# Layer norm 2's root by Pool as a power, a new interleave over four PSUM slots, and down sums in another order

## The chip, the cores and the metric

The kernel runs on one core of a Trainium2 chip. The metric is the device time of one execution in microseconds (us). PE is the tensor engine, DVE the vector engine, ACT the scalar engine, POOL the GpSimd engine, SP the engine that issues most DMAs. A profile's span is about 2 us shorter than the time of the same execution.

## The reference

```python
x = A_x                                            # 2048 x 576
h = x + spectral(layernorm(x), A_w_r, A_w_i)       # 2-D FFT, filter, inverse FFT, to bf16
h2 = h + (gelu(n @ w_gate) * (n @ w_up)) @ w_down  # n = layernorm(h); 4608 hidden columns
```

Layer norm has eps = 1e-5 and no weights.

## The kernel before: the parts that matter here

The 2048 rows are 16 tiles of 128. The program is recorded operation by operation: each engine runs its operations in the order of recording, and the recorder adds the semaphore waits. The spectral part ends with an inverse transform. For a tile `c`, `I` makes a half-transformed tile in PSUM (six matmuls) and ACT moves it to `GS`; `N` multiplies by the second table (four matmuls) and DVE adds it to the residual `XO`, with the row sum as accumulator:

```python
def st_N(c):
    ...                                                    # 4 matmuls into two PSUM banks
    P.op(DVE, ... scalar_tensor_tensor(x2, banks(...), 1.0, x2, op0=mult, op1=add,
                                       accum_out=SB2[:, 0, c:c + 1]), ...)
```

Eight tiles are inverted before the feed-forward part starts. Layer norm 2 of the first block (tiles 0 to 3, in the groups 0-2 and 3) needs sums, squares (ACT, `sq`), a root, the norm itself, and a transpose by matmul ("turn") into `HT`. Its root was taken on two engines, and the sequence was written by hand:

```python
def ln2_b(q):   # ACT
    a.activation(RS2[:, c0:c1], RS2[:, c0:c1], ACTF.Sqrt, bias=EPT[:, 0:1])
def ln2_c(q):   # DVE
    v.reciprocal(RS2[:, c0:c1], RS2[:, c0:c1])

# ... cut: I0 to s2
ln2_a(0); st_I(5); ln2_b(0); st_N(4); sq(3); ln2_c(0)
norm(0, DVE); norm(1, POOL); norm(2, POOL)
ln2_a(1); st_I(6); ln2_b(1); st_N(5); st_I(7); ln2_c(1); norm(3, DVE)
turn_pe(0, ACT); st_N(6); turn_pe(1, DVE); turn_pe(2, ACT); turn_pe(3, ACT); st_N(7)
```

A PSUM slot is two banks. Inverses and turns alternated between slots 0 and 1, `N` steps between slots 2 and 3. After that come four blocks of 512 rows. Each has 36 gate/up steps `f` (18 matmuls, then Gelu on ACT and a product on DVE into `AT`), and then the down sums over `f`. In blocks 1 to 3 the gate/up steps run in the order 9 to 35, then 0 to 8, but the sums ran from 0 to 35:

```python
for h, (d0, d1) in enumerate(((0, cut), (cut, D))):
    b = (0, 1, 2, 3)[2 * (p % 2) * (tb > 0) + h]
    ...
    for f in range(36):
        ...
        t.matmul(bank(b, 0, 128, 0, d1 - d0), AT[:, f, ...], WD[:, f, d0:d1], start=(f == 0), stop=(f == 35))
    P.op(DVE, ... tensor_tensor(OS[...], bank(b, ...), XO[:, c, d0:d1], op=add), ...)
```

Of the kernel before, what the change touches and what calls it, by code (L numbers as in the profile page):

```python
# [5 lines left out]
F32 = mybir.dt.float32  # L6
# [8 lines left out]
NT = 16  # L15
# [2 lines left out]
NPAIR = 18  # L18
EPS = 1e-5
NPRE = 8  # L20


def _np_bf16(a):
# [286 lines left out]
def _build(nc, A_x, A_w_r, A_w_i, B_w_gate, B_w_up, B_w_down, out):  # L310
# [40 lines left out]
    TM = sb.alloc("TM", [128, 2, NT], F32)  # L351
    RS2 = sb.alloc("RS2", [128, NT], F32)
    EPT = sb.alloc("EPT", [128, 1], F32)
    OS = sb.alloc("OS", [128, 2, D], BF16)
    shared = (sb.off + 63) // 64 * 64

# [42 lines left out]
    def banks(b, n, w):  # L399
        return PS[:, b * 512:(b + n) * 512].rearrange("p (a c) -> p a c", a=n)[:, :, 0:w]  # L400


    P.op(POOL, lambda g: g.memset(ZD[:, :], 0.0), w=["ZD"])
    P.op(POOL, lambda g: g.memset(EPT[:, :], EPS), w=["EPT"])
    P.op(POOL, lambda g: g.memset(WS[:, :, :, 0:KW:K2], 0.0), w=["Wz"])
    xv = A_x[0].rearrange("(p c) d -> p c d", c=NT)
# [353 lines left out]
    vkeys = vk[0] + vk[1] + vk[2]  # L760


    ISEQ = [("I", c) for c in range(8)] + [("T", i) for i in range(4)]
    seq = {k: i % 2 for i, k in enumerate(ISEQ)}

    def islot(c):
        return seq["I", c]

    def i_mm(c, h, i):
        b, kt = 2 * islot(c) + h, 2 * i + h  # L770
        P.op(PE, lambda t, b=b, h=h, i=i, kt=kt, c=c: t.matmul(bank(b, 0, 128, 0, K2), V[:, c, kt, :, :], DT[:, 3 * h + i, 0:K2],  # L771
                                                              start=(i == 0), stop=(i == 2)), r=vk[i] + ["DT"], w=[("PS", b)])

    def i_ev(c):
        sl, b0 = c % 2, 2 * islot(c)
        if c == 0:
            P.op(DVE, lambda v, sl=sl, b0=b0: v.tensor_copy(GS[:, sl, 0, 0:K2], bank(b0, 0, 128, 0, K2)), r=[("PS", b0)], w=[("G", sl, 0)])
            P.op(ACT, lambda a, sl=sl, b0=b0: a.activation(GS[:, sl, 1, 0:K2], bank(b0 + 1, 0, 128, 0, K2), ACTF.Copy), r=[("PS", b0 + 1)], w=[("G", sl, 1)])
        else:
            P.op(ACT, lambda a, sl=sl, b0=b0: a.activation(GS[:, sl, :, 0:K2], banks(b0, 2, K2), ACTF.Copy),  # L780
                 r=[("PS", b0), ("PS", b0 + 1)], w=[("G", sl, 0), ("G", sl, 1)])


    def st_I01():
        for c in range(2):
            for h in range(2):
                i_mm(c, h, 0)
        for c in range(2):
            for h in range(2):
                for i in (1, 2):  # L790
                    i_mm(c, h, i)
            i_ev(c)
# [11 lines left out]
    def st_N(c):  # L804
        sl = c % 2
        for h in range(2):
            b = 4 + 2 * sl + h
            for i in range(2):
                rhs = GS[:, sl, i, 288:0:-1] if h else GS[:, sl, i, 0:288]
                P.op(PE, lambda t, b=b, h=h, i=i, c=c, rhs=rhs: t.matmul(bank(b, 0, 128, 0, 288), IT[:, h * i, c, :], rhs, start=(i == 0), stop=(i == 1)),  # L810
                     r=[("G", sl, i), "IT"], w=[("PS", b)])
        x2 = XO[:, c, 0:D].rearrange("p (a b) -> p a b", a=2)
        P.op(DVE, lambda v, x2=x2, c=c, sl=sl: v.scalar_tensor_tensor(x2, banks(4 + 2 * sl, 2, 288), 1.0, x2, op0=ALU.mult, op1=ALU.add,  # L813
                                                               accum_out=SB2[:, 0, c:c + 1]),
             r=[("PS", 4 + 2 * sl), ("PS", 5 + 2 * sl)], w=[("X", c), ("S0", c)])


    QR = ((0, 3), (3, 4), (4, NPRE), (NPRE, NT))

    def ln2_a(q):  # L820
        c0, c1 = QR[q]
        P.op(DVE, lambda v, c0=c0, c1=c1: v.tensor_scalar(TM[:, 1, c0:c1], SB2[:, 0, c0:c1], -1.0 / D, None, op0=ALU.mult), r=[("S0", c) for c in range(c0, c1)], w=[("MN", q)])
        P.op(DVE, lambda v, c0=c0, c1=c1: v.tensor_tensor(TM[:, 0, c0:c1], TM[:, 1, c0:c1], TM[:, 1, c0:c1], op=ALU.mult), r=[("MN", q)], w=[("M2", q)])
        P.op(DVE, lambda v, c0=c0, c1=c1: v.scalar_tensor_tensor(RS2[:, c0:c1], SB2[:, 1, c0:c1], 1.0 / D, TM[:, 0, c0:c1], op0=ALU.mult, op1=ALU.subtract),
             r=[("M2", q)] + [("S1", c) for c in range(c0, c1)], w=[("V2", q)])

    def ln2_b(q):
        c0, c1 = QR[q]
        P.op(ACT, lambda a, c0=c0, c1=c1: a.activation(RS2[:, c0:c1], RS2[:, c0:c1], ACTF.Sqrt, bias=EPT[:, 0:1]), r=[("V2", q), "EPT"], w=[("SD2", q)])

    def ln2_c(q):
        c0, c1 = QR[q]
        P.op(DVE, lambda v, c0=c0, c1=c1: v.reciprocal(RS2[:, c0:c1], RS2[:, c0:c1]), r=[("SD2", q)], w=[("RS2", q)])

    def lq(c):
        return sum(c >= q0 for q0, _ in QR) - 1
# [17 lines left out]
    def turn_pe(c, eng):  # L854
        hs = c % 4
        t0, t1 = 128 * c, 128 * c + 128
        b0 = 2 * seq["T", c]
        for k in range(5):
            b, o = b0 + k // 4, 128 * (k % 4)
            lhs = HN[:, hs, 128 * k:128 * k + 128]  # L860
            P.op(PE, lambda t, b=b, o=o, lhs=lhs: t.matmul(bank(b, 0, 128, o, o + 128), lhs, IDT[:, :], start=True, stop=True),
                 r=[("HN", hs, 0), ("HN", hs, 1), "IDT"], w=[("PS", b)])
        dst, src = HT0[:, 0:5, t0:t1], PS[:, b0 * 512:b0 * 512 + 640].rearrange("p (k e) -> p k e", k=5)
        fn = (lambda a: a.activation(dst, src, ACTF.Copy)) if eng == ACT else (lambda v: v.tensor_copy(dst, src))  # L864
        P.op(eng, fn, r=[("PS", b0), ("PS", b0 + 1)], w=[("HT", 0, c, 0)])

    def sq(c):
        square(c, OS[:, c % 2, :], ("OS", c % 2, 0))

    st_I01()  # L870
    st_N(0)
    st_I(2)
    st_N(1)
    sq(0)
    st_I(3)
    st_N(2)
    sq(1)
    st_I(4)
    st_N(3)
    sq(2)  # L880
    ln2_a(0)
    st_I(5)
    ln2_b(0)
    st_N(4)
    sq(3)
    ln2_c(0)
    norm(0, DVE)
    norm(1, POOL)
    norm(2, POOL)
    ln2_a(1)  # L890
    st_I(6)
    ln2_b(1)
    st_N(5)
    st_I(7)
    ln2_c(1)
    norm(3, DVE)
    turn_pe(0, ACT)
    st_N(6)
    turn_pe(1, DVE)
    turn_pe(2, ACT)  # L900
    turn_pe(3, ACT)
    st_N(7)

    P.alias(ukeys + [(n_, a) for n_ in ("CU", "SU") for a in range(3)], [("WD", j) for j in range(9)])
    for j in range(9):
# [68 lines left out]
    def down(tb, p):  # L974
        c = 4 * tb + p

        cut = 448 if c == NT - 1 else 288
        for h, (d0, d1) in enumerate(((0, cut), (cut, D))):
            b = (0, 1, 2, 3)[2 * (p % 2) * (tb > 0) + h]
            cd = NPRE + 2 * p + h if tb == 0 else NT  # L980
            if cd < NT:
                def_i(cd)
            for f in range(36):
                if cd < NT and f == 22:
                    def_n(cd)
                P.op(PE, lambda t, b=b, d0=d0, d1=d1, f=f, p=p: t.matmul(bank(b, 0, 128, 0, d1 - d0), AT[:, f, 128 * p:128 * p + 128],  # L986
                                                                        WD[:, f, d0:d1], start=(f == 0), stop=(f == 35)),
                     r=[("AT", f), ("WD", f // 4)], w=[("PS", b)])
            P.op(DVE, lambda v, b=b, d0=d0, d1=d1, p=p, c=c: v.tensor_tensor(OS[:, p % 2, d0:d1], bank(b, 0, 128, 0, d1 - d0), XO[:, c, d0:d1], op=ALU.add),  # L989
                 r=[("PS", b), ("X", c)], w=[("OS", p % 2, k) for k in (range(2) if d1 == cut and cut > 288 else (h,))])  # L990
            P.dma(SP, ov[:, c, d0:d1], OS[:, p % 2, d0:d1], f"so{p % 2}{h}", r=[("OS", p % 2, h)], w=[("OUT", p % 2, h)])


    P.alias(fdead, fnew)
    for tb in range(4):
        for f in range(36):
            gu_part(36 * tb + f, False)
            if f:
                gu_part(36 * tb + f - 1, True)
            if tb == 0 and f == 10:  # L1000
                wg_load(3, 0)
            if tb == 0 and f < NPRE - 4:
                sq(4 + f)
            if tb == 0 and f == 8:
                ln2_a(2)
                ln2_b(2)
                ln2_c(2)
            f0, f1 = (15, 3) if tb == 0 else (2, 4)
            if tb < 3 and f >= f0 and (f - f0) % f1 == 0 and (f - f0) // f1 < 4:
                norm(4 * (tb + 1) + (f - f0) // f1)  # L1010
                turn_dma(4 * (tb + 1) + (f - f0) // f1)
        gu_part(36 * tb + 35, True)
        for p in range(4):
            down(tb, p)
        if tb == 0:
            ln2_a(3)
            ln2_b(3)
            ln2_c(3)
            P.alias(vkeys + ["DP", "ITD", "EB", "Q0", "Q1", "YB0", "YB1", "JD"], [("WG", 3, k) for k in range(4)])
            wg_load(0, 3)  # L1020
    P.op(SP, None, r=[("OUT", i, h) for i in range(2) for h in range(2)])
# [36 lines left out]
```

## Time and profile before

Time before: 501.41 us, median of 3 runs (501.16 to 501.94); with a fourth run, 501.5. I cut the span by marks that the chain of waits and the timeline show: the first matmul of the inverse transform, the first gate/up matmul, and the start of each later block. The last come from the chain of waits and lie up to 0.07 us after a block's first matmul; block 1 before is counted from its second matmul, the first that had to wait.

| part of the span before | from, to (us) | length |
|---|---|---|
| up to the first inverse matmul | 0 to 53.16 | 53.16 |
| transition: inverse, layer norm 2, turns | 53.16 to 67.21 | 14.05 |
| block 0 | 67.21 to 179.36 | 112.15 |
| blocks 1, 2, 3 | 179.36, 285.41, 391.39 to 497.49 | 106.05, 105.98, 106.10 |

From the page of the kernel before: span, busy time by engine, and the chain of waits summed by engine.

```profile
span 499.7 us, 9895 instructions
PE 487.6 (98%) x4322; PEld 290.5 (58%) x4323; DVE 197.3 (39%) x431; ACT 159.4 (32%) x299; POOL 37.4 (7%) x51
PE 88%; DVE 8%; issue 2%; ACT 1%; DMA 1%; DVEq 0%; ACTq 0%
```

PE is busy nearly all the time, so only its gaps can be won. The chain of waits of the kernel before, in order of time (start, length, engine, tile, line, count), shows where it left PE:

```profile
59.26 0.77 DVE XO L813 x2
...
61.39 1.08 DVE HN L842 x2
...
65.08 0.75 DVE HT L864
65.87 0.47 PE PS L861 x5
66.36 0.71 ACT HT L864
67.08 0.14 issue
67.21 70.11 PE PS L936 x648
...
178.84 0.47 DVE OS L989
179.36 70.11 PE PS L936 x647
249.56 0.61 ACT GL L945
250.19 0.70 DVE AT L946
250.93 34.47 PE PS L986 x280
```

The reader should see three places: the transition (to 67.21), an output add before block 1 (178.84), and a Gelu and a product inside a down sum (249.56), which comes back at the other two blocks. PE's own waits in the same trace (who waited for whom, us in total, times, longest) for the lines concerned:

```profile
PE PS L986 <- DVE AT L946: 1.2, 3, 0.4
PE PS L861 <- DVE HT L864: 0.8, 1, 0.8
PE PS L936 <- DVE OS L989: 0.3, 1, 0.3
```

These waits are shorter than the time lost, since a matmul's recorded end is modelled and lies after its last issue. Eight matmuls at 0.123 us from 249.39 end their issue at 250.37; the ninth started at 250.93. So 0.55 us is lost there, where the view says 0.4.

### The profile page before, as it was taken

The numbers are of one execution on the slowest core, as the hardware profiler recorded it, in microseconds if no ns is written. First come the engines' busy times: TensorE is split into PE (matmuls) and PEld (weight loads), VectorE is DVE, ScalarE is ACT, GpSimd is POOL, SyncE is SP. The second block draws the span as 40 slices with busy tenths as digits, with TensorE's granted clock in tenths as the row PEclk, the third lists the DMA queues.
The fourth block names the chain that finished last, engine by engine and source line by source line (L and its number), as shares of the span: only waits on it lengthen the run. The fifth ranks groups of instructions, "written<-read, shape, count | busy, mean of one in ns | idle before, by whom it ended". The sixth has DMA issues, their size and how long they took to land.

```text
span 499.7 us, 9895 instructions
## 1 busy us (share of the span) xinstructions
PE 487.6 (98%) x4322; PEld 290.5 (58%) x4323; DVE 197.3 (39%) x431; ACT 159.4 (32%) x299; POOL 37.4 (7%) x51
## 2 busy tenths in 40 slices
PE   6999989999999999999999999999999999999998
PEld 2688745555588854444477744444577544444775
DVE  5899743443365544433311134433210233333111
ACT  7888765332321242323300023323100133233000
POOL 3653260000000010000000000000000000000000
PEclk9899999999999999999999999999999999999999
DMA  8765796511000052100000001100000000000000
GB/s 281 169 206 183 253 354 250 210 26 26 7 13 13 14 182 65 25 9 1 2 13 19 18 14 22 20 1 1 7 12 19 13 1 1 1 2 1 12 19 19
DMA packets 27163, 31.32 MB, mean 63 GB/s; under 512 B 11664, under 2 KB 19984, under 8 KB 27120
## 3 DMA queue, kind: packets, MB, share of 16 engines
q1 hardware_dynamic: 24224, 18.75, 13.0%
q0 software_dynamic: 2896, 11.95, 6.8%
q8 instruction: 34, 0.56, 0.5%
q14 instruction: 9, 0.07, 0.1%
HBM read 26.35 MB, written 2.36 MB: 57 GB/s over the span
## 4 chain that ended last, share of the span: by engine, by line
PE 88%; DVE 8%; issue 2%; ACT 1%; DMA 1%; DVEq 0%; ACTq 0%
PE PS L936 56%; PE PS L986 28%; DVE TP L667 2%; DVE ST L468 1%; PE PS L953 1%; PE PS L771 1%; DVE ZS L672 1%; DVE CUS L641 1%; PE PS L691 1%; DMA XO<-in_A_x_dram 1%; DVE XO L813 1%; PE PS L628 1%; DVE U L533 0%; DVE AT L946 0%; PE PS L810 0%
## 5 line engine op out<-in xcount | busy, mean ns | idle before, releaser
L936 PE MATMUL PS<-HT,WG 64*128 64x512 bf16 x2106 | 229.1, 376 | 0.7 <-ACT HT L864 0.4
L936 PEld LDWEIGHTS PS<-HT,WG 64*128 64x128 bf16 x2106 | 107.7, 94 | 120.4 <-issue 1.4
L946 DVE TENSOR_TENSOR AT<-GL,PS 128x512 bf16<-128x512 bf16 x144 | 99.0, 688 | 176.4 <-ACT GL L945 176.4
L945 ACT ACTIVATE GL<-PS 128x512 bf16<-128x512 f32 x144 | 85.9, 597 | 258.5 <-PE PS L936 246.4
L986 PE MATMUL PS<-WD,AT 128*128 128x288 bf16 (+2 forms) x1152 | 144.8, 286 | 1.2 <-DVE AT L946 1.2
L986 PEld LDWEIGHTS PS<-WD,AT 128*128 128x128 bf16 x1152 | 110.5, 98 | 32.6 <-DVE AT L946 2.1
L989 DVE TENSOR_TENSOR OS<-PS,XO 128x288 bf16<-128x288 f32 (+2 forms) x32 | 14.6, 458 | 102.0 <-PE PS L986 102.0
L936 PE MATMUL PS<-HT,WGX 64*128 64x512 bf16 x486 | 53.8, 376 | 0.0
L936 PEld LDWEIGHTS PS<-HT,WGX 64*128 64x128 bf16 x486 | 23.8, 94 | 28.8
L712 POOL TENSOR_SCALAR WS<-WS 128x290 bf16<-128x290 bf16 x16 | 15.4, 963 | 9.2 <-DMA WS<-in_A_w_i_dram 5.4
L628 PE MATMUL PS<-FT,U 128*128 128x290 bf16 x96 | 14.4, 287 | 0.5 <-DVE U L533 0.5
L801 ACT ACTIVATE JD<-XO 128x576 bf16<-128x576 bf16 x8 | 5.5, 683 | 28.5 <-DVE XO L970 28.5
L667 DVE TENSOR_TENSOR TP<-YS,WS 128x580 bf16<-128x580 bf16 (+2 forms) x32 | 13.4, 459 | 0.3 <-issue 0.3
L691 PE MATMUL PS<-VT,ZS 128*128 128x256 bf16 x102 | 13.5, 272 | 0.0
L704 ACT ACTIVATE V<-PS 128x768 bf16<-128x768 f32 x15 | 12.0, 811 | 0.8 <-PE PS L691 0.6
L660 ACT ACTIVATE YS<-PS 128x578 bf16<-128x578 f32 x16 | 10.5, 655 | 3.5 <-PE PS L657 3.3
L657 PE MATMUL PS<-CUS,BT 128*128 128x289 bf16 (+2 forms) x96 | 10.7, 246 | 0.3 <-DVE CUS L641 0.3
L522 PE MATMUL PS<-ATS,XO 128*128 128x128 bf16 (+1 forms) x80 | 7.3, 238 | 3.8 <-POOL ATS L495 2.3
L628 PEld LDWEIGHTS PS<-FT,U 128*128 128x128 bf16 x96 | 9.2, 98 | 3.0 <-issue 0.6
L691 PEld LDWEIGHTS PS<-VT,ZS 128*128 128x128 bf16 x102 | 9.2, 98 | 1.8 <-DVE ZS L672 0.2
L468 DVE BATCH_NORM_STATS2 ST<-XO 128x6 f32<-128x288 bf16 x22 | 8.4, 445 | 3.8 <-DMA XO<-in_A_x_dram 3.8
L657 PEld LDWEIGHTS PS<-CUS,BT 128*128 128x128 bf16 x96 | 8.3, 97 | 2.1 <-issue 0.5
(75 smaller groups left out, 201.2 us busy)
## 6 DMA issues: line engine op xcount, KB each, us to landing
WD<-in_B_w_down_dram POOLq DMA_DIRECT2D x9, 576.0 KB, 11.6
WG<-in_B_w_up_dram SPq DMA_DIRECT2D x4, 1152.0 KB, 6.6
WG<-in_B_w_gate_dram POOLq DMA_DIRECT2D x4, 1152.0 KB, 9.8
out_dram<-OS SPq DMA_DIRECT2D x30, 72.0 KB, 1.6
XO<-in_A_x_dram SPq DMA_DIRECT2D x3, 576.0 KB, 7.3
WGX<-in_B_w_gate_dram POOLq DMA_DIRECT2D x1, 1152.0 KB, 6.7
WGX<-in_B_w_up_dram SPq DMA_DIRECT2D x1, 1152.0 KB, 11.1
HT<-HN SPq DMA_TRANSPOSE x60, 2.4
```

Of the source, the lines that this page charges most:

```text
L468: P.op(DVE, lambda v, c=c, h=h: v.bn_stats(ST1[:, c, h, :], XO[:, c, 288 * h:288 * h + 288]), r=[("X", c)], w=[("ST1", c, h)])
L628: P.op(PE, lambda t, b=b, o=o, dt=dt, us=us, g=g: t.matmul(bank(b, 0, 128, 0, 2 * HK), U[:, us, g, :, :], FT[:, o, dt, :], start=(dt == 0) ...
L657: P.op(PE, lambda t, b=b, tb=tb, pl=pl, q0=q0, q1=q1, m=m, s3=s3, sp_=sp_: t.matmul(bank(b, 0, 128, q0, q1), BT[:, sp_, tb, :], CUS[:, s3, ...
L667: P.op(DVE, lambda v: v.tensor_tensor(out, YS[:, sl, :, q0:q1], WS[:, g, w_, q0:q1], op=ALU.mult), r=[("Y", sl), ("Wn", i), "Yz", "Zz"] + ...
L691: P.op(PE, lambda t, b=b, o=o, zp=zp, lhs=lhs, sp_=sp_, m=m, n=len(parts): t.matmul(bank(b, 0, 128, o, o + 256), lhs, VT[:, sp_, zp, :], s ...
L704: P.op(ACT, lambda a, dst=dst, src=src: a.activation(dst, src, ACTF.Copy), r=[("PS", bs[0]), ("PS", bs[2])], w=[("V", g, c) for c in range ...
L712: P.op(POOL, lambda v, g=GORD[i]: v.tensor_scalar(WS[:, g, 0, :], WS[:, g, 2, :], -1.0, None, op0=ALU.mult), r=[k for k in wkeys[0 if 1 <= ...
L936: op = P.op(PE, lambda t, h0=h0, kt=kt, wt=wt, b=b, s=(not second and j == 0), e=(second and j == n - 1): t.matmul(bank(b), wg_tile(slot)[ ...
L945: P.op(ACT, lambda a: a.activation(GL[:, s2, :], bank(b0), ACTF.Gelu_apprx_tanh), r=[("PS", b0)], w=[("GL", s2)])
L946: P.op(DVE, lambda v: v.tensor_tensor(AT[:, f, :], GL[:, s2, :], bank(b0 + 1), op=ALU.mult), r=[("GL", s2), ("PS", b0 + 1)], w=[("AT", f)])
L986: P.op(PE, lambda t, b=b, d0=d0, d1=d1, f=f, p=p: t.matmul(bank(b, 0, 128, 0, d1 - d0), AT[:, f, 128 * p:128 * p + 128], WD[:, f, d0:d1], ...
L989: P.op(DVE, lambda v, b=b, d0=d0, d1=d1, p=p, c=c: v.tensor_tensor(OS[:, p % 2, d0:d1], bank(b, 0, 128, 0, d1 - d0), XO[:, c, d0:d1], op=A ...
```

## The change

Its intent is to close these gaps. The root becomes one POOL operation (power -0.5); the groups of layer norm 2 become tiles 0-1 and 2-3; both POOL norms go to DVE; inverses, `N` steps and turns are interleaved anew and go round four PSUM slots in turn; the last down sums of block 0 use banks 6 and 7; the down sums of blocks 1 to 3 follow the order in which their inputs are made.

```diff
+QR = ((0, 2), (2, 4), (4, NPRE), (NPRE, 16))
+SEQ = """I0 I1 N0 I2 N1 s0 m0 I3 s1 N2 r0 I4 N3 s2 n0 I5 m1 s3 N4 r1 A0 I6 n1 n3 n2 N5 I7 D3 A1 z2 N6 N7""".split()
...
+    P.op(POOL, lambda g: g.memset(EXQ[:, :], -0.5), w=["EXQ"])
...
-    seq = {k: i % 2 for i, k in enumerate(ISEQ)}
+    SLOT = {k: 2 * ((v - len(SLOT)) % 4) for k, v in SLOT.items()}
...
+        P.op(DVE, ... tensor_scalar(TM[:, 0, c0:c1], TM[:, 0, c0:c1], EPS, None, op0=ALU.subtract) ...)
-        P.op(ACT, ... activation(RS2[:, c0:c1], RS2[:, c0:c1], ACTF.Sqrt, bias=EPT[:, 0:1]) ...)
-        P.op(DVE, ... reciprocal(RS2[:, c0:c1], RS2[:, c0:c1]) ...)
+        P.op(POOL, ... tensor_tensor(RS2[:, c0:c1], RS2[:, c0:c1], EXQ[:, c0:c1], op=ALU.pow) ...)
...
-            b = (0, 1, 2, 3)[2 * (p % 2) * (tb > 0) + h]
+            b = (0, 1, 2, 3)[2 * (p % 2) * (tb > 0) + h] if tb or p < 3 else 6 + h
-            for f in range(36):
+            for f in [*range(36)] if tb == 0 else [*range(9, 36), *range(9)]:
```

In `SEQ`, `I`, `N` and `s` are inverse, N step and square of a tile; `m` and `r` the mean part and the root of a group; `n` a norm on DVE; `A`, `D`, `z` a turn evicted by ACT, by DVE, or by both.

More of the change, by code (lines that the diff above doesn't have):

```diff
@@ L353, in _build @@
     EPT = sb.alloc("EPT", [128, 1], F32)
+    EXQ = sb.alloc("EXQ", [128, NT], F32)
     OS = sb.alloc("OS", [128, 2, D], BF16)
@@ L760, in _build @@
     vkeys = vk[0] + vk[1] + vk[2]
-    ISEQ = [("I", c) for c in range(8)] + [("T", i) for i in range(4)]
-    seq = {k: i % 2 for i, k in enumerate(ISEQ)}
-    def islot(c):
-        return seq["I", c]
+    SLOT = {}
+    for w in SEQ:
+        if w[0] in "INADz":
+            SLOT["T" if w[0] in "ADz" else w[0], int(w[1:])] = len(SLOT)
+    SLOT = {k: 2 * ((v - len(SLOT)) % 4) for k, v in SLOT.items()}
     def i_mm(c, h, i):
-        b, kt = 2 * islot(c) + h, 2 * i + h
+        b, kt = SLOT["I", c] + h, 2 * i + h
         P.op(PE, lambda t, b=b, h=h, i=i, kt=kt, c=c: t.matmul(bank(b, 0, 128, 0, K2), V[:, c, kt, :, :], DT[:, 3 * h + i, 0:K2],
@@ L774, in i_ev @@
     def i_ev(c):
-        sl, b0 = c % 2, 2 * islot(c)
+        sl, b0 = c % 2, SLOT["I", c]
         if c == 0:
@@ L806, in st_N @@
         for h in range(2):
-            b = 4 + 2 * sl + h
+            b = SLOT["N", c] + h
             for i in range(2):
@@ L812, in st_N, with ln2_m @@
         x2 = XO[:, c, 0:D].rearrange("p (a b) -> p a b", a=2)
-        P.op(DVE, lambda v, x2=x2, c=c, sl=sl: v.scalar_tensor_tensor(x2, banks(4 + 2 * sl, 2, 288), 1.0, x2, op0=ALU.mult, op1=ALU.add,
+        P.op(DVE, lambda v, x2=x2, c=c, sl=sl: v.scalar_tensor_tensor(x2, banks(SLOT["N", c], 2, 288), 1.0, x2, op0=ALU.mult, op1=ALU.add,
                                                                accum_out=SB2[:, 0, c:c + 1]),
-             r=[("PS", 4 + 2 * sl), ("PS", 5 + 2 * sl)], w=[("X", c), ("S0", c)])
-    QR = ((0, 3), (3, 4), (4, NPRE), (NPRE, NT))
-    def ln2_a(q):
+             r=[("PS", SLOT["N", c]), ("PS", SLOT["N", c] + 1)], w=[("X", c), ("S0", c)])
+    def ln2_m(q):
         c0, c1 = QR[q]
@@ L823, in ln2_a, with ln2_r @@
         P.op(DVE, lambda v, c0=c0, c1=c1: v.tensor_tensor(TM[:, 0, c0:c1], TM[:, 1, c0:c1], TM[:, 1, c0:c1], op=ALU.mult), r=[("MN", q)], w=[("M2", q)])
+        P.op(DVE, lambda v, c0=c0, c1=c1: v.tensor_scalar(TM[:, 0, c0:c1], TM[:, 0, c0:c1], EPS, None, op0=ALU.subtract), r=[("M2", q)], w=[("M3", q)])
+    def ln2_r(q):
+        c0, c1 = QR[q]
         P.op(DVE, lambda v, c0=c0, c1=c1: v.scalar_tensor_tensor(RS2[:, c0:c1], SB2[:, 1, c0:c1], 1.0 / D, TM[:, 0, c0:c1], op0=ALU.mult, op1=ALU.subtract),
-             r=[("M2", q)] + [("S1", c) for c in range(c0, c1)], w=[("V2", q)])
-    def ln2_b(q):
-        c0, c1 = QR[q]
-        P.op(ACT, lambda a, c0=c0, c1=c1: a.activation(RS2[:, c0:c1], RS2[:, c0:c1], ACTF.Sqrt, bias=EPT[:, 0:1]), r=[("V2", q), "EPT"], w=[("SD2", q)])
-    def ln2_c(q):
-        c0, c1 = QR[q]
-        P.op(DVE, lambda v, c0=c0, c1=c1: v.reciprocal(RS2[:, c0:c1], RS2[:, c0:c1]), r=[("SD2", q)], w=[("RS2", q)])
+             r=[("M3", q)] + [("S1", c) for c in range(c0, c1)], w=[("V2", q)])
+        P.op(POOL, lambda g, c0=c0, c1=c1: g.tensor_tensor(RS2[:, c0:c1], RS2[:, c0:c1], EXQ[:, c0:c1], op=ALU.pow), r=[("V2", q), "EXQ"], w=[("RS2", q)])
     def lq(c):
@@ L856, in turn_pe @@
         t0, t1 = 128 * c, 128 * c + 128
-        b0 = 2 * seq["T", c]
+        b0 = SLOT["T", c]
+        kd = 3 if eng is None else 4
         for k in range(5):
-            b, o = b0 + k // 4, 128 * (k % 4)
+            b, o = b0 + k // kd, 128 * (k % kd)
             lhs = HN[:, hs, 128 * k:128 * k + 128]
@@ L862, in turn_pe @@
                  r=[("HN", hs, 0), ("HN", hs, 1), "IDT"], w=[("PS", b)])
-        dst, src = HT0[:, 0:5, t0:t1], PS[:, b0 * 512:b0 * 512 + 640].rearrange("p (k e) -> p k e", k=5)
-        fn = (lambda a: a.activation(dst, src, ACTF.Copy)) if eng == ACT else (lambda v: v.tensor_copy(dst, src))
-        P.op(eng, fn, r=[("PS", b0), ("PS", b0 + 1)], w=[("HT", 0, c, 0)])
+        for e, k0, k1, q0 in ((ACT, 0, 3, 0), (DVE, 3, 5, 512)) if eng is None else ((eng, 0, 5, 0),):
+            dst, src = HT0[:, k0:k1, t0:t1], PS[:, b0 * 512 + q0:b0 * 512 + q0 + 128 * (k1 - k0)].rearrange("p (k e) -> p k e", k=k1 - k0)
+            fn = (lambda a, dst=dst, src=src: a.activation(dst, src, ACTF.Copy)) if e == ACT else (lambda v, dst=dst, src=src: v.tensor_copy(dst, src))
+            P.op(e, fn, r=[("PS", b0 + q0 // 512)] + ([("PS", b0 + 1)] if eng else []), w=[("HT", 0, c, k0)])
     def sq(c):
         square(c, OS[:, c % 2, :], ("OS", c % 2, 0))
+    RUN = {"I": st_I, "N": st_N, "s": sq, "m": ln2_m, "r": ln2_r, "n": norm, "p": lambda c: norm(c, POOL), "A": lambda c: turn_pe(c, ACT), "D": lambda c: turn_pe(c, DVE),
+           "z": lambda c: turn_pe(c, None)}
     st_I01()
-    st_N(0)
-    st_I(2)
-    st_N(1)
-    sq(0)
-    st_I(3)
-    st_N(2)
-    sq(1)
-    st_I(4)
-    st_N(3)
-    sq(2)
-    ln2_a(0)
-    st_I(5)
-    ln2_b(0)
-    st_N(4)
-    sq(3)
-    ln2_c(0)
-    norm(0, DVE)
-    norm(1, POOL)
-    norm(2, POOL)
-    ln2_a(1)
-    st_I(6)
-    ln2_b(1)
-    st_N(5)
-    st_I(7)
-    ln2_c(1)
-    norm(3, DVE)
-    turn_pe(0, ACT)
-    st_N(6)
-    turn_pe(1, DVE)
-    turn_pe(2, ACT)
-    turn_pe(3, ACT)
-    st_N(7)
+    for w in SEQ[2:]:
+        RUN[w[0]](int(w[1:]))
     P.alias(ukeys + [(n_, a) for n_ in ("CU", "SU") for a in range(3)], [("WD", j) for j in range(9)])
@@ L986, in down @@
                 P.op(PE, lambda t, b=b, d0=d0, d1=d1, f=f, p=p: t.matmul(bank(b, 0, 128, 0, d1 - d0), AT[:, f, 128 * p:128 * p + 128],
-                                                                        WD[:, f, d0:d1], start=(f == 0), stop=(f == 35)),
+                                                                        WD[:, f, d0:d1], start=(f == 9 * (tb > 0)), stop=(f == (8 if tb else 35))),
                      r=[("AT", f), ("WD", f // 4)], w=[("PS", b)])
@@ L1004, in _build @@
             if tb == 0 and f == 8:
-                ln2_a(2)
-                ln2_b(2)
-                ln2_c(2)
+                ln2_m(2)
+                ln2_r(2)
             f0, f1 = (15, 3) if tb == 0 else (2, 4)
@@ L1015, in _build @@
         if tb == 0:
-            ln2_a(3)
-            ln2_b(3)
-            ln2_c(3)
+            ln2_m(3)
+            ln2_r(3)
             P.alias(vkeys + ["DP", "ITD", "EB", "Q0", "Q1", "YB0", "YB1", "JD"], [("WG", 3, k) for k in range(4)])
```

## The prediction

> **What bounds it now.** The tensor engine: the page has it busy 98% of 499.7 us at a granted clock of 0.997, and it is 88% of the chain of waits. Only its gaps can be won. By the chain and the timeline:
> 1. Transition (inverse transform, layer norm 2, turns, first gate/up), 53.16 to 67.21 us. One inverse takes 0.75 us, one N step 0.49. Back to back from the first N step at 54.84: 8x0.49 + 6x0.75 + 4x0.27 (turns) = 9.5 us, so 64.3; the stage ends at 67.21. Loss 2.9 us, behind norm 0, PSUM reuse and two slow Pool norms (3.05 us the pair).
> 2. Down sums of blocks 1 to 3: eight matmuls (0.123 us each) run, then the ninth waits for the Gelu (0.61) and product (0.70) computed last (f=8): 249.39 + 0.98 = 250.37, resumed 250.93. Lost 0.55 each, 1.65 in all.
> 3. Block 0's last down sum to block 1's gate/up: the bank is held until the output add ends; second matmul at 179.36 where 178.78 was due: 0.58.
>
> **What changes.**
> - Gap 2: sums start at f=9 and end at f=8, so the last product has 35 matmuls' time. All 1.65 gone.
> - Gap 3: block 0's last sum uses banks 6 and 7, wanted only four steps later. 0.58 gone.
> - Transition: Sqrt on the scalar engine (0.30) and reciprocal (0.17, queued behind an add) give way to one Pool power on 128x2. The Pool norms go to the vector engine, where one takes 0.63 without Pool beside it (1.08 with). One more small subtract per group (0.2). The vector queue is then the limit. From its fourth add's end at 60.02: norm 0.64, mean group 0.55, add 0.76, variance 0.16, three norms 1.92, add 0.8, turn copies 0.82 and 0.42 = 6.1, so gate/up at about 66.2 if the power takes at most 0.6. Win 1.0, not 2.9. The tensor engine waits about 0.4 for norm 0, 0.5 for norm 3, 0.8 for the slot of add 5.
> - The power's time is in no trace here; the Trainium skill, "GPSIMD Engine Reference", section "2.1 Instruction dispatch", says only that instructions pass software dispatch and a per-core loop. The trace's small Pool operations take 0.10 (memset, one column) to 0.48 (norm, 64 columns). My estimate: 0.5 to 1.0 us. Each 0.1 above 0.6 costs 0.1, above 0.75 costs 0.2. I put 0.7 us on the transition.
> - Groups 2 and 3 lose their Sqrt and two table loads each: 1.283 us each in the trace, as "ScalarE: Activation LUTs", section "What ACT_TABLE_LOAD costs", states. No tensor wait stands there: 0. The down weights load some 1.5 us earlier; used at 138: 0.
>
> **Sum.** 501.4 - 1.65 - 0.58 - 0.7 = 498.5 us. Range 497.3 to 500.1. Faster by over 2%: 1%; within 2%: 98%; slower: 1%.
>
> **What would show it.** No wait of down-sum matmuls on the product, none of gate/up on the output add; blocks 1 to 3 each 0.55 shorter; first gate/up at 66.2 to 66.9; vector engine nearly gapless from 60 to 66; four Pool powers under 1 us; table loads from six to two.
>
> **What would make it wrong.** A power of 2 us or more (first use, or element by element) would stall the vector queue twice and lose about 1.7 us in the transition: about 500.9. Overlap that makes the vector queue shorter than I add up would win up to 1 us more.

## The result, and the profile after

The changed kernel took 497.93 us, median of 4 runs (497.79 to 498.12), against 501.5 (4 runs, 501.16 to 501.94). A ratio here is the mean time of one kernel's runs over that of the other's of the same rounds, so not quite the ratio of the medians quoted. It is 0.9928, 95% interval 0.9911 to 0.9946: a gain of 3.6 us. The range, 497.3 to 500.1, holds it.

| part of the span | before | after | gained |
|---|---|---|---|
| up to the first inverse matmul | 53.16 | 53.04 | 0.12 |
| transition | 14.05 | 12.85 | 1.20 |
| block 0 (to 179.36; to 177.41) | 112.15 | 111.52 | 0.63 |
| block 1 (to 285.41; to 282.84) | 106.05 | 105.43 | 0.62 |
| block 2 (to 391.39; to 388.26) | 105.98 | 105.42 | 0.56 |
| block 3 (to 497.49; to 493.79) | 106.10 | 105.53 | 0.57 |

The gains add up to the 3.7 us between the spans. (Because of the marks named above, some 0.06 us of block 1's gain belongs to the output add before it. The chain below starts gate/up at 65.95, where the modelled end of the matmul before it lies; its first matmul started at 65.89, as the table has it.) The 0.12 in the first row is no gain of the change: that mark lies between 52.7 and 53.6 us over all the kernels, whose first part is the same but for a few small operations.

The page and the chain of waits of the changed kernel, same views as before:

```profile
span 496.0 us, 9895 instructions
PE 487.7 (98%) x4323; PEld 285.5 (58%) x4323; DVE 198.0 (40%) x436; ACT 153.3 (31%) x291; POOL 39.6 (8%) x52
```

```profile
61.75 0.83 POOL RS L833
62.60 1.49 DVE HN L842 x4
64.09 0.38 DVE XO L817 x2
64.47 0.05 issue
64.52 0.45 PE PS L862 x5
64.97 0.99 PE PS L814 x8
65.95 70.04 PE PS L910 x648
...
177.41 70.04 PE PS L910 x648
247.45 35.39 PE PS L960 x288
282.84 70.04 PE PS L910 x648
```

The output add, the Gelu and the product have left the chain: from one gate/up stage to the next there is nothing but PE. What is left in the transition is in PE's waits, of which these three concern the turns:

```profile
PE PS L862 <- DVE HN L842: 0.4, 1, 0.4
PE PS L862 <- DVE XO L817: 0.3, 1, 0.3
PE PS L862 <- DVE TM L825: 0.3, 1, 0.3
```

The first is the turn behind norm 3, the second a turn that needs the slot of add 5. The third is the first turn, which reads norm 0; the view names the small DVE operation that follows that norm. The prediction had 0.5, 0.8 and 0.4 for them.

The timeline of the changed kernel (start, length, engine, line, operation, count, idle before and releaser) shows the same three on DVE's side. Lines of other engines are left out except POOL's powers and the issue of the down weights:

```profile
59.00 0.72 POOL L833 TENSOR_TENSOR RS<-RS,EXQ 128x2 f32<-128x2 f32 x1 [4.05 <-DVE RS L831]
59.14 0.76 DVE L817 SCALAR_TENSOR_TENSOR XO<-PS,XO 128x576 bf16<-128x576 f32 x1 [0.23 <-PE PS L814]
...
59.82 0.64 DVE L842 TENSOR_SCALAR HN<-XO,TM,RS 128x576 bf16<-128x576 bf16 x2
...
61.58 0.64 DVE L842 TENSOR_SCALAR HN<-XO,TM,RS 128x576 bf16<-128x576 bf16 x2
...
61.75 0.82 POOL L833 TENSOR_TENSOR RS<-RS,EXQ 128x2 f32<-128x2 f32 x1 [2.02 <-DVE RS L831]
...
62.52 6.76 POOL L222 DMA_DIRECT2D WD<-in_B_w_down_dram  x9
62.60 1.49 DVE L842 TENSOR_SCALAR HN<-XO,TM,RS 128x576 bf16<-128x576 bf16 x4 [0.38 <-POOL RS L833]
...
63.70 0.75 DVE L817 SCALAR_TENSOR_TENSOR XO<-PS,XO 128x576 bf16<-128x576 f32 x1
```

A norm is two instructions here (x2), on 576 and 64 columns (the last 64 again, into the padding). The first power ends at 59.72, just before norm 0 starts (59.82). The second holds DVE for 0.38 us before norm 3. Then note a thing that matters later: the two norms from 62.60 are recorded as 1.49 us, but the next DVE operation starts after 1.10.

### The profile page after: what moved, and what is told of

The parts are those of the page before. It is cut to its first block, busy times and chain, and to the rows that moved or that the text cites. A ratio compares the mean times of both kernels' runs of the same rounds, so it can differ in the third digit from the quotient of the medians.

```text
span 496.0 us, 9895 instructions
## 1 busy us (share of the span) xinstructions
PE 487.7 (98%) x4323; PEld 285.5 (58%) x4323; DVE 198.0 (40%) x436; ACT 153.3 (31%) x291; POOL 39.6 (8%) x52
## 4 chain that ended last, share of the span: by engine, by line
PE 89%; DVE 7%; issue 2%; DMA 1%; ACT 1%; POOL 0%; DVEq 0%
PE PS L910 56%; PE PS L960 29%; DVE TP L671 2%; DVE ST L472 1%; DVE CUS L645 1%; PE PS L927 1%; PE PS L775 1%; DVE ZS L676 1%; PE PS L695 1%; PE PS L814 1%; DMA XO<-in_A_x_dram 1%; PE PS L632 1%; DVE U L537 0%; DVE HN L842 0%; PE PS L941 0%
## 5 line engine op out<-in xcount | busy, mean ns | idle before, releaser
L910 PEld LDWEIGHTS PS<-HT,WG 64*128 64x128 bf16 x2106 | 102.2, 94 | 124.8 <-issue 0.9
L833 POOL TENSOR_TENSOR RS<-RS,EXQ 128x2 f32<-128x2 f32 (+2 forms) x4 | 4.2, 1060 | 113.3 <-DVE RS L831 113.3
L842 DVE TENSOR_SCALAR HN<-XO,TM,RS 128x576 bf16<-128x576 bf16 (+1 forms) x32 | 10.4, 372 | 0.4 <-POOL RS L833 0.4
L515 PE MATMUL PS<-ZD 128*128 128x512 bf16 x24 | 9.1, 537 | 1.3 <-POOL ZD L406 1.3
```

The lines of the kernel that those rows point to most:

```text
L910: op = P.op(PE, lambda t, h0=h0, kt=kt, wt=wt, b=b, s=(not second and j == 0), e=(second and j == n - 1): t.matmul(bank(b), wg_tile(slot)[ ...
```

## The experiments

Three builds failed and never ran: the power on DVE, alone or with the eps added in the same instruction, did not compile, and the same fused form on POOL was refused as outside its operations. "Stage" in the table is the transition, from the first inverse matmul to the first gate/up matmul, read from each run's timeline.

| run | what it is | time, median (us) | ratio to before, 95% | stage (us) |
|---|---|---|---|---|
| before | | 501.5 | | 14.05 |
| changed | | 497.93 | 0.9928 (0.9911 to 0.9946) | 12.85 |
| e1_order | before + order of the down sums | 499.77 | 0.9967 (0.9955 to 0.9980) | 14.05 |
| e2_banks | before + banks 6 and 7 | 500.86 | 0.9986 (0.9974 to 0.9999) | 14.05 |
| e3_trans | changed, without these two | 500.29 | 0.9979 (0.9966 to 0.9993) | 12.85 |
| e4_sqrt | changed, Sqrt + reciprocal | 498.44 | 0.9943 (0.9929 to 0.9956) | 13.21 |
| e5_powonly | before + power only | 504.76 | 1.0067 (1.0052 to 1.0082) | 15.78 |
| e6_slots | changed, old slot rule | 499.45 | 0.9957 (0.9943 to 0.9971) | 14.47 |
| e7_twice | changed, every power twice | 499.41 | 0.9956 (0.9942 to 0.9969) | 14.32 |
| e10_seq | changed, new sequence, norm 0 on POOL | 497.71 | 0.9922 (0.9909 to 0.9934) | 12.44 |
| e11_seq3 | changed, new sequence, all norms on DVE | 497.79 | 0.9926 (0.9912 to 0.9939) | 12.50 |
| e12_held | changed, down weights issued later | 497.99 | 0.9928 (0.9916 to 0.9941) | 12.86 |
| e13_both | e11 and e12 together | 497.35 | 0.9918 (0.9905 to 0.9932) | 12.25 |
| e14_sqheld | e4 and e12 together | 497.98 | 0.9930 (0.9916 to 0.9943) | 12.90 |

The intervals are about 0.6 to 0.9 us wide to each side, so differences of a few tenths are read from the stage in the traces, one trace for each kernel. Kernels with the same transition have it alike to 0.01 us (before, e1 and e2; changed and e3). All results were correct.

### e1_order, e2_banks, e3_trans: do the parts add up?

```diff
-            for f in range(36):
+            for f in [*range(36)] if tb == 0 else [*range(9, 36), *range(9)]:
-   start=(f == 0), stop=(f == 35)
+   start=(f == 9 * (tb > 0)), stop=(f == (8 if tb else 35))
```

> The kernel before with only the down sums of blocks 1 to 3 taken in the order f=9..35, 0..8. Theory (the parts add up, each gap is its own): blocks 1, 2 and 3 each 0.55 us shorter, nothing else moves, so 501.5 - 1.65 = 499.8 us; no wait of a down-sum matmul on the gate product is left. Rival (most of the gain is in the transition): under 0.7 us.

```diff
-            b = (0, 1, 2, 3)[2 * (p % 2) * (tb > 0) + h]
+            b = (0, 1, 2, 3)[2 * (p % 2) * (tb > 0) + h] if tb or p < 3 else 6 + h
```

> The kernel before with only block 0's last down sums in banks 6 and 7. Theory: the wait of block 1's first gate/up on the output add goes, 0.58 us, so 500.9 us. Rival (the profile shows the wait as 0.3 us, so the gap is only that): 501.2 us.

The third undoes both edits in the changed kernel.

> The changed kernel with the old order of the down sums and the old banks, so only the transition (power, interleave, four slots) is new. Theory: first gate/up at 65.9 us as in the changed kernel, all else as before, so 1.2 to 1.3 us gain over before: 500.2 us. Rival (the earlier start is given back later, by the down weights' loads or the norms of block 1): under 0.5 us gain.

Against before's median of the same rounds, 501.49, they gained 1.72, 0.63 and 1.20 us. That is 3.55 together, and the whole change gained 3.57. So within the noise the parts add up, all three theories held, and none of the rivals. The second also settles how to read PE's wait of 0.3 us on the output add: the gap was worth about 0.6. The chain of e2 shows it gone, with block 1 starting 111.52 us after block 0, where before had 112.15:

```profile
67.08 70.11 PE PS L936 x648
178.60 70.05 PE PS L936 x648
```

In e3 nothing of the transition's 1.20 us was given back later.

### e5_powonly and e6_slots: which part of the transition is it?

e5 puts the power (with its subtract) into the kernel before, in the places of Sqrt and reciprocal, and changes nothing else.

> The kernel before with the power on Pool in place of Sqrt and reciprocal, and nothing else of the change: old sequence, two Pool norms. Theory (the power is worth something only in the new interleave): the second group's power queues on Pool behind the two Pool norms (3 us), norm 3 starts near 65.6 instead of 63.8 us, first gate/up near 69.3 instead of 67.2: about 2 us slower than before, 503.5 us. Rival (the power alone wins by leaving out a hop between engines): 500.3 to 501.0 us.

```profile
61.46 2.90 POOL L845 TENSOR_SCALAR HN<-XO,TM,RS 128x576 bf16<-128x576 bf16 x4
64.52 0.55 POOL L832 TENSOR_TENSOR RS<-RS,EXQ 128x1 f32<-128x1 f32 x1 [0.15 <-POOL HN L845]
65.11 0.72 DVE L845 TENSOR_SCALAR HN<-XO,TM,RS 128x576 bf16<-128x576 bf16 x2 [1.26 <-POOL RS L832]
```

As these lines of its timeline show, the second power stands behind the two POOL norms, and norm 3 waits 1.26 us for it. The stage is 1.73 us longer than before (theory: about 2). The profiled execution took 503.16 us, near the 503.5 expected, but the other three took 504.5 to 505.5. No trace shows where these lost more, and that stays open; the sign is not in doubt.

```diff
     SLOT = {k: 2 * ((v - len(SLOT)) % 4) for k, v in SLOT.items()}
+    ts = [k for k in SLOT if k[0] == "T"]
+    SLOT = {k: 4 + 2 * (k[1] % 2) if k[0] == "N" else 2 * (k[1] % 2) if k[0] == "I" else 2 * (ts.index(k) % 2) for k in SLOT}
```

> The changed kernel with the old PSUM rule: inverses and turns alternate between two slots, N steps between the other two. Theory (the four rotating slots carry part of the gain): inverse 6 waits for the eviction of turn 0, about 1 us, and later turns wait for the eviction of inverse 7 and turn 3: 1 to 2 us slower than the changed kernel, 499.0 to 500.0 us, so that most of the transition's gain is gone. Rival (the order alone is enough, since the vector queue is the limit): within 0.3 us of 497.9.

The stage grew from 12.85 to 14.47 us, longer than in the kernel before (14.05). So the new order needs other slots than the old ones; over those it loses. Where it loses is in the timeline of e6: inverse 6 waits for the eviction of turn 0, and a turn waits for the eviction of inverse 7.

```profile
61.70 0.92 PE L777 MATMUL PS<-DT,V 128*128 128x289 bf16 x6 [0.80 <-ACT HT L868]
64.61 0.73 PE L864 MATMUL PS<-IDT,HN 128*128 128x128 bf16 x10 [0.75 <-ACT GS L786]
```

### e7_twice: is the power's length on the path?

```diff
+        P.op(POOL, ... tensor_tensor(RSX[:, c0:c1], RS2[:, c0:c1], EXQ[:, c0:c1], op=ALU.pow) ...)
         P.op(POOL, ... tensor_tensor(RS2[:, c0:c1], RS2[:, c0:c1], EXQ[:, c0:c1], op=ALU.pow) ...)
```

> The changed kernel with every power done twice on Pool (first into a tile nobody reads). Each small power takes 0.72 to 0.82 us in the changed kernel's trace. Theory (the prediction's: above about 0.75 us each group's power stands in the vector queue, so both excesses count): norm 0 about 0.7 us later and norm 3 about 0.75 us more, so about 1.5 us slower, 499.4 us. Rival (Pool has slack): within 0.3 us of 497.9. Between (only the second group counts): 0.7 to 0.9 us slower.

The time rose by 1.48 us and the stage by 1.47, from 12.85 to 14.32. Both groups count, as the prediction said: DVE waits 0.63 us for the first power and 1.15 for the second, where it waited 0 and 0.38.

```profile
60.41 0.64 DVE L844 TENSOR_SCALAR HN<-XO,TM,RS 128x576 bf16<-128x576 bf16 x2 [0.63 <-POOL RS L835]
63.96 1.49 DVE L844 TENSOR_SCALAR HN<-XO,TM,RS 128x576 bf16<-128x576 bf16 x4 [1.15 <-POOL RS L835]
```

### e4_sqrt, e12_held, e14_sqheld: is the power better than Sqrt and reciprocal?

```diff
-        P.op(POOL, ... tensor_tensor(RS2[:, c0:c1], RS2[:, c0:c1], EXQ[:, c0:c1], op=ALU.pow) ...)
+        P.op(ACT, ... activation(RS2[:, c0:c1], RS2[:, c0:c1], ACTF.Sqrt) ...)
+        P.op(DVE, ... reciprocal(RS2[:, c0:c1], RS2[:, c0:c1]) ...)
```

> The changed kernel with the Pool power replaced, in the same place of the sequence, by Sqrt on the scalar engine and the reciprocal on the vector engine. Theory (the interleave won the transition, and the power only keeps the scalar and vector queues free): the vector queue stands about 0.35 us at each of the two reciprocals, and the scalar engine's evictions come 0.5 to 0.9 us later: 0.5 to 1.0 us slower than the changed kernel, so 498.4 to 498.9 us, still well below before. Rival (the power itself is the gain): 1.2 us slower or more, at 499.1 us or above. Second rival (the power is no help): within 0.2 us of 497.9.

It came out 0.5 us slower, and 0.36 us longer in the stage, as the theory had it. But its timeline showed a second cause mixed in:

```profile
56.47 5.20 POOL L222 DMA_DIRECT2D WD<-in_B_w_down_dram  x7
57.47 0.48 DVE L825 TENSOR_SCALAR TM<-SB 128x2 f32<-128x2 f32 x1
60.11 0.83 DVE L843 TENSOR_SCALAR HN<-XO,TM,RS 128x576 bf16<-128x576 bf16 x2
```

With nothing else to do, POOL issues the loads of the down weights 7.6 us sooner, counted from the first inverse (from 54.95 on; the line above shows the part after 56), beside DVE's small operations. Some of these slow down: 0.48 us for 0.17, and 0.83 for a norm of 0.64. All that did are TENSOR_SCALAR instructions; the product of two SBUF inputs kept its 0.16 both times. The Trainium skill, "GPSIMD Engine Reference", section "8. Key points", says that POOL shares its SBUF interfaces with the vector engine, with contention against vector instructions in a 2-port mode or with two SBUF inputs; these numbers agree that they disturb each other, in this case to the vector engine's cost, though not that every operation with two SBUF inputs suffers. The DMA traffic itself is no rival cause: from 56 to 62 us the DMA engines are as busy in e14 below (a share of 1.02 to 1.08), where these loads are held back, as in e4 (1.04 to 1.06). So I held the loads back in both variants, until the last turn was evicted; they are first used some 70 us later.

```diff
-        P.dma(POOL, WD[:, 4 * j:4 * j + 4, :], wdv[...], f"wd{j}", w=[("WD", j)])
+        P.dma(POOL, WD[:, 4 * j:4 * j + 4, :], wdv[...], f"wd{j}", r=[("HT", 0, 2, 3)], w=[("WD", j)])
```

> The changed kernel with the issue of the down weights' loads held on Pool until the last turn is evicted; they are first used some 70 us later. Theory (Pool's issuing of these loads slows the vector engine's norms 3 and 2, 1.49 us for the two against 1.27 uncontended, on the limiting queue): the two norms take 1.27, first gate/up 0.2 us sooner, 12.6 to 12.7 us for the stage, 497.7 us. Rival (the two norms are slow for another reason, or the queue does not limit): no change, 12.85 us.

> Sqrt and reciprocal in place of the power, with the down weights' loads held as in the run above, so that Pool is idle beside the vector engine in both. In the earlier Sqrt run Pool issued the loads 6 us sooner and slowed the vector engine's small operations (0.48 for 0.16 us), so the power's worth was mixed with that. Theory: by itself the power is worth 0.2 to 0.3 us: 0.2 to 0.3 us longer for the stage than with the power and held loads. Rival (the 0.5 us of the earlier run was the hops between engines): 0.4 us or more. Second rival (all of it was the loads): under 0.1 us.

My theory of e12 failed. The two norms did get shorter, from 1.49 to 1.19 us, but the stage stayed at 12.86:

```profile
62.30 1.19 DVE L842 TENSOR_SCALAR HN<-XO,TM,RS 128x576 bf16<-128x576 bf16 x4 [0.38 <-POOL RS L833]
63.40 0.75 DVE L817 SCALAR_TENSOR_TENSOR XO<-PS,XO 128x576 bf16<-128x576 f32 x1
```

The next DVE operation starts 1.10 us after the first norm in both kernels. Only the landing of the last norm moved, and the turn that reads it waits for the slot of add 5 anyway. The theory of e14 failed too: with the loads held, Sqrt and reciprocal cost the stage 0.04 us more than the power (12.90 and 12.86), and the times are equal (497.98 and 497.99). Its second rival stands: what e4 lost was the earlier loads. The power as such gains at most a few hundredths here. It takes longer than the two operations that it replaces: the root is ready 1.06 us after the variance's start in the changed kernel (61.51 to 62.57), 0.59 in e14 (61.41 to 62.00). But during it DVE runs norm 1, which needs only the first root, and in e14 DVE waits for Sqrt and does the reciprocal before norm 1. So norm 3 starts about equally late, 1.09 and 1.04 us after the variance (in e14 at 62.45, the second norm of the last line):

```profile
61.41 0.16 DVE L831 SCALAR_TENSOR_TENSOR RS<-SB,TM 128x2 f32<-128x2 f32 x1
61.92 1.72 DVE L843 TENSOR_SCALAR HN<-XO,TM,RS 128x576 bf16<-128x576 bf16 x6
```

One thing is left open. e4 and e14 keep the power's extra subtract (0.17 us), which Sqrt with its bias would not need. No run leaves it out. The trace of e14 allows little for it: the square of tile 3 ends at 61.35, so this variance could start at most 0.06 us sooner.

### e10_seq, e11_seq3, e13_both: a better sequence?

`N` is split into its matmuls (`M`) and its add (`x`), and the slots are shifted by one: `2 * ((v - len(SLOT) - 1) % 4)`. `p` is a norm on POOL.

```diff
-SEQ = """... N3 s2 n0 I5 m1 s3 N4 r1 A0 I6 n1 n3 n2 N5 I7 D3 A1 z2 N6 N7"""
+SEQ = """... N3 s2 p0 m1 s3 I5 N4 r1 I6 n1 N5 A0 n3 n2 I7 A1 M6 D3 z2 x6 N7"""   # e10
+SEQ = """... N3 s2 n0 I5 m1 s3 N4 r1 I6 n1 N5 A0 n3 n2 I7 A1 M6 A3 z2 x6 N7"""   # e11, e13
```

> The changed kernel with a new sequence: norm 0 on Pool between the two powers, the variance of group 1 earlier (square 3 before inverse 5's eviction), turn 0 after N step 5, add 5 before norm 3, N step 6 before turn 3 with its add after the turns' evictions, slots shifted by one. Theory (the vector queue between add 3 and the last turn's eviction is the limit, and Pool beside adds costs nothing): the vector queue loses norm 0 (0.64) and the wait for the second power (0.38); first gate/up at 65.1 to 65.4 us instead of 65.9, so 497.2 to 497.5 us. Rival (Pool's norm slows the vector engine or its own power, or the scalar engine is the limit): within 0.2 us of 497.9 or slower.

The stage fell by 0.41 us to 12.44, less than the 0.5 to 0.8 that I wanted; the time, 497.71, missed the 497.2 to 497.5 expected and is not clear of the changed kernel's. The timeline tells why: DVE's small two-input product took 0.51 us for 0.16 while POOL ran norm 0 (contention again, the skill's two-SBUF-input case), and N step 5 waited for inverse 5's eviction.

```profile
59.51 1.32 POOL L849 TENSOR_SCALAR HN<-XO,TM,RS 128x576 bf16<-128x576 bf16 x2
59.83 0.51 DVE L833 TENSOR_TENSOR TM<-TM 128x2 f32<-128x2 f32 x1
61.00 0.67 PE L814 MATMUL PS<-GS,IT 128*128 128x288 bf16 x4 [0.22 <-ACT GS L784]
```

> The changed kernel with the sequence of the run before but norm 0 back on the vector engine, inverse 5 and square 3 in the old order, and turn 3 evicted by the scalar engine. Theory (a Pool norm beside the vector engine's small two-input operation cost 0.35 us there, and the wait for inverse 5's eviction some more; without both, the add of tile 5 fills the wait for the second power): from the first inverse to the first gate/up 12.3 to 12.5 us (changed kernel 12.85, last run 12.44), 497.4 to 497.6 us. Rival (Pool's norm was worth its 0.64 us): longer than 12.44 us.

It gave 12.50 us in the stage, and 497.79 us, which misses the 497.4 to 497.6 expected. The stage is at the edge of both texts, so the run does not tell whether the POOL norm was worth having.

> Both of the two runs before it: new sequence and held loads. Theory: 12.2 to 12.4 us for the stage, 497.2 to 497.4 us, the fastest of all. Rival (another engine is the limit by now): no better than the sequence alone.

12.25 us, as expected, and at 497.35 us the lowest median of all (three of its four runs 497.27 to 497.43; the fourth, the profiled one, 497.92, with a first inverse matmul at 53.61). Here the held loads are worth 0.25 us, where in e12 they were worth none: in this sequence add 5 stands before the last two norms, so the landing of the last norm is what its turn waits for. In the stage it is 0.6 us ahead of the changed kernel; the intervals of the two times overlap widely, so the gain in time is likely, not proven.

## Why the prediction was right

- **PE bounds, only its gaps count.** Right: PE is busy 487.6 us before and 487.7 after, and the span fell by the gaps alone.
- **Gap 2, order of the down sums, 1.65 us.** Measured alone 1.72 in time, and blocks 1 to 3 are 0.56 to 0.62 us shorter in the changed kernel.
- **Gap 3, banks 6 and 7, 0.58 us.** Measured alone 0.63.
- **Transition, 0.7 us.** Measured 1.20. This is the term that was mis-sized, and nearly the whole difference between 498.5 and 497.9. The order of events was right up to add 5: norm 0 does not wait for the first power, norm 3 waits 0.38 us for the second (I expected about 0.5 for the matmuls behind it), and one turn waits for the slot of add 5. The size failed in the sum over the vector queue. I added recorded lengths: 0.64 for a norm, 1.92 for three. The trace shows a norm followed by the next norm or the next add after 0.55, and an add followed after about 0.68 where its record says 0.75. The Trainium skill, "Perfetto Trace Analysis", section "Optimizing Scalar/DVE Operations", says so: the write-acknowledgement half of a profiled latency overlaps with the next instruction. Four norms at 0.09 us less nearly make up for the 0.38 us that DVE waits. From the fourth add's end to that of add 5 I had 4.83 us; the trace has 4.57 (59.90 to 64.47), the wait included. On top I had subtracted 0.3 us for a slow power. The last piece was not what I had summed: I added DVE's turn copies (0.82 and 0.42), but by the chain it is PE that ends last, with a turn (0.45) and N steps 6 and 7 (0.99).
- **The power, estimated 0.5 to 1.0 us.** It took 0.72 and 0.82 for two columns. The slope (0.2 us for each 0.1 above 0.75) is about what e7 showed: 1.47 us for two powers that each became ready some 0.8 us later.
- **What I credited to the power was not its own.** The prediction told of the power as if it freed time. e14 shows that Sqrt and reciprocal in the same sequence are as good. The interleave with four slots won the 1.20 us, taken as a whole with the new groups and the norms moved to DVE: the order without the slots is 1.62 us longer (e6), and the power without the order costs 1.73 (e5). The four slots under the old order, and the groups or the moved norms alone, were not tried.
- **Table loads, 0.** Right. They went from six to two, 1.283 us each in the trace, which is the load time that "ScalarE: Activation LUTs", section "What ACT_TABLE_LOAD costs", states, and e3's block 0 (66.08 to 178.23, 112.15 us) is as long as before's 112.15.
- **Earlier down weights, 0.** Right for this kernel (e12: no change), though for a reason that I had not seen: they do disturb DVE, at a point where nothing waits. In e4 and e11 the same loads cost 0.3 and 0.25 us.

## What to carry to other kernels

Where an engine is busy 98% of the span, list its gaps by the chain of waits, and measure each from the issue that was due to the issue that came; here the repairs added up. A sum should start with the input that was ready first, and a buffer should be one that the next stage wants last. Add up a queue by start-to-start distances, not by recorded lengths. When an operation is moved to another engine, look at what that engine does next: here the timing of POOL's DMA issues was worth more (0.25 to 0.3 us of the stage) than the operation that had been moved (0.04).

## What the Trainium skill lacked or had wrong

- "GPSIMD Engine Reference" has no cost for the power. Recorded here (the profiler's spans on POOL are rough) on 128 partitions in fp32: 0.55 us for one column and 0.89 for three (e5), 0.72 and 0.82 for two, 1.03 for four, 1.67 for eight, so about 0.16 us for each further column between one and eight.
- The same page (section "8. Key points") names the contention with the vector engine without a size. Here a two-column DVE operation went from 0.16 or 0.17 us to 0.48 beside POOL's issuing of DMAs and to 0.51 beside a POOL norm, and a norm from 0.64 to 0.83. This is about that page alone: "SBUF — State Buffer" treats the shared ports further, with no size for these operations.
- "Perfetto Trace Analysis", section "Optimizing Scalar/DVE Operations", puts the profiled latency at about twice the engine's own access overhead. That concerns the overhead, not the operation, and the page has no figure for a queue. Here a norm of 0.64 us overlapped with the next operation by 0.09, and an add of 0.75 by about 0.07; so for these the queue is shorter than the sum of its records by some 10 to 15%.
- No page read says that a PE wait read from modelled matmul ends understates the loss. Here 0.4 us stood for 0.55 and 0.3 for 0.6.
